# Transposes of the reciprocal row sums issued one step later in both batches of a sliding-window attention, with the broadcast load and the normalisation behind them in the second

## The chip, the cores and the metric

The kernel runs on one core of one Trainium2 chip. The metric is the device time of one execution in microseconds (us). The kernel before takes 372.78 us, the median of 3 runs (372.46 to 373.1).

## The reference

Three blocks are chained: attention with a sliding window and four sink columns, an MLP with a convolution over three tokens and a gate, and attention in four experts weighted by a top-2 gate. The change touches the first block alone, where B=2, H=8, S=768, D=64 and the window is 128:

```python
scores = scale * np.matmul(q, k.transpose(0, 1, 3, 2))
keep = is_sink | in_window
scores = np.where(keep, scores, -1000000000.0)
scores = scores - np.max(scores, axis=-1, keepdims=True)
a = np.exp(scores)
a = a / (np.sum(a, axis=-1, keepdims=True) + 1e-09)
return np.matmul(a, v)
```

Its output x, as (2, 768, 512), goes into the MLP: `h = relu(x @ w_in)`, the convolution over three neighbouring tokens, `h * sigmoid(conv)`, and `@ w_out`.

## The kernel before, in words

The attention works on tiles of 128 queries (`qt`, six to a batch) and pairs of heads (`pr`, four to a tile), so 24 steps to a batch. Each step sends one pair through a chain of stages. Each stage is a small method that issues instructions, and a table gives its lag in steps. `run_phases` (L46) puts the call of stage i at step floor(lag + i times rate) and issues the calls step by step; inside a step the table `ORD1` (L78) sets the order of the stages. Batch 0 is phase `a0`, batch 1 is phase `a1` and begins 24 steps later at a rate of 1.1 steps to a pair; from step 30 on the MLP (stages `m.*`) runs between its steps. Each engine works through its own queue strictly in the order of issue, so the tables set the order of the work on TensorE (PE), VectorE (DVE), ScalarE (ACT), GpSimd (POOL), and on SyncE (SP), which issues the DMAs.

For each pair the stages are:
- S (`a1_S`, L449): matmuls of the scores (L484, in batch 1 L471), mask and minimum on DVE (L486), exponentials on ACT with the row sums into the tile `su` (L489).
- T (L532): PE transposes P (L545), and ACT copies the result into PT (L501).
- V (L576): matmuls of PT with v (L587) into a bank of PSUM that the tile's four pairs share; the sink columns are added by L595, after a transpose L567, a copy SPT (L569) and a product on DVE (L574).

Once for each tile of queries:
- r (L494): 1/(row sum + eps) on DVE, L496 and L497.
- rT (L511): PE transposes `su`, 128x8, into 8x128 (L514); ACT (batch 0, L501) or DVE (batch 1, L503) copies it to the tile rT; a DMA stores it to `rD` in DRAM (L518).
- rB (L520): two loads, L525, read `rD` back, spread over the 128 partitions, into the tile R.
- xm (`x_norm`, L527): DVE multiplies the output in PSUM by R (L529), which frees that bank.
- xh (L611), xl (L614) and halo (L619): the normalised x is split into two parts, xh by a cast on ACT (L501) and xl on DVE (L617), and POOL fills the edges (L623, L626). The MLP's first matmuls, L753, read both parts.

The MLP's stages are H (L753, with the relu's eviction L756 on ACT), the convolution (L766, L767 on DVE, the sigmoid L769 on ACT), the gate (L774 on DVE, L776 on ACT, the product g on POOL, L782) and Y (L797). In the background, whenever a step has credit for it, weights are decoded on DVE (L343, L346, L349, L413, L509) and ACT (L339, L507), and L372 loads the raw weights, 512 KB each, through SP.

PSUM is handed out as eight banks. A new tile gets the bank that has been free for longest and waits for its last reader.

The line that the change touches is the table of lags, L74, one row to a batch. Its first column is the lag of r, and its columns 8 to 13 are the lags of rB, rT, xm, xh, xl and halo, in this order:

```python
LAGS = ((1, 2, 1, 4, 3, 4, 5, 5, 2, 7, 7, 9, 11), (1, 1, 2, 6, 3, 4, 5, 3, 2, 5, 6, 7, 7))
```

Of the kernel before, what the change touches and what calls it, by code (L numbers as in the profile page):

```python
# [70 lines left out]
BG0 = 550  # L71
BG1 = 650
BG2 = 1200
LAGS = ((1, 2, 1, 4, 3, 4, 5, 5, 2, 7, 7, 9, 11), (1, 1, 2, 6, 3, 4, 5, 3, 2, 5, 6, 7, 7))  # L74
LAGM = (1, 2, 3)
A2_N = 2
EVT = 'aaadadada'
# [11 lines left out]
class Kernel:  # L89
# [1033 lines left out]
    def program(self, general):  # L1123
# [5 lines left out]
        with ExitStack() as ctx:  # L1129
# [34 lines left out]
            else:  # L1164
# [18 lines left out]
                self.fixed()  # L1183
                first = [self.attn_phase(b, b * NSTEP, LAGS[b], self.attn_misc(b)) for b in range(B)]
                m1 = NSTEP + MLP_START
# [109 lines left out]
```

## Time and profile before

| | |
|---|---|
| median of 3 runs | 372.78 us (372.46 to 373.1) |
| the profiled execution | 372.33 us, of which the profile's span is 370.5 us |
| PE busy | 359.5 us, 97% of the span |
| DVE busy | 272.3 us, 73% |
| ACT busy | 264.3 us, 71% |
| POOL busy | 118.5 us, 32% |

The profile is of one execution; its times are in us from the span's start. Attention of batch 0 fills the stretch to about 60 us, that of batch 1 runs beside the MLP until about 170 us, and the MoE attention follows behind the MLP. A row of a timeline reads: start, duration, engine, line, operation, the tile written and the tiles read, count, and in brackets how long the engine had been idle and on what it had waited.

### The profile page before, as it was taken

The numbers are of one execution on the slowest core, as the hardware profiler recorded it, in microseconds if no ns is written. First come the engines' busy times: TensorE is split into PE (matmuls) and PEld (weight loads), VectorE is DVE, ScalarE is ACT, GpSimd is POOL, SyncE is SP. The second block draws the span as 40 slices with busy tenths as digits, with TensorE's granted clock in tenths as the row PEclk, the third lists the DMA queues.
The fourth block names the chain that finished last, engine by engine and source line by source line (L and its number), as shares of the span: only waits on it lengthen the run. The fifth ranks groups of instructions, "written<-read, shape, count | busy, mean of one in ns | idle before, by whom it ended". The sixth has DMA issues, their size and how long they took to land.

```text
span 370.5 us, 8892 instructions
## 1 busy us (share of the span) xinstructions
PE 359.5 (97%) x3166; PEld 331.7 (90%) x3166; DVE 272.3 (73%) x834; ACT 264.3 (71%) x778; POOL 118.5 (32%) x230
## 2 busy tenths in 40 slices
PE   7999999899999999999999999999999999999995
PEld 5687877899899999999999999999999899978984
DVE  5689899999887997878756756139668688578631
ACT  4999998766886766546746866249888698759841
POOL 7014120444432442844421222500034144406310
PEclk9999999999999999999999999999999999999999
DMA  7944765353342300001211010000000000001102
GB/s 181 355 138 131 243 208 181 115 189 125 105 125 70 104 30 31 9 21 29 59 44 44 1 58 3 0 2 0 2 3 1 30 30 28 31 1 58 59 32 93
DMA packets 20404, 27.53 MB, mean 74 GB/s; under 512 B 2080, under 2 KB 12928, under 8 KB 20352
## 3 DMA queue, kind: packets, MB, share of 16 engines
q1 hardware_dynamic: 19120, 26.22, 22.3%
q10 hardware_dynamic: 1232, 0.66, 0.8%
q8 instruction: 27, 0.44, 0.5%
q14 instruction: 25, 0.20, 0.2%
HBM read 23.68 MB, written 3.19 MB: 73 GB/s over the span
## 4 chain that ended last, share of the span: by engine, by line
PE 73%; DVE 14%; ACT 6%; issue 2%; POOL 2%; DMA 1%; ACTq 0%; DVEq 0%
PE psB L797 15%; PE psB L753 14%; PE psB L947 9%; PE psB L1071 5%; PE psB L875 5%; PE psB L1047 4%; PE psB L587 4%; PE psB L1095 3%; PE psB L484 3%; PE psB L545 3%; DVE P L486 3%; PE psB L1010 2%; PE psB L1009 2%; PE psB L471 2%; ACT P L489 2%
## 5 line engine op out<-in xcount | busy, mean ns | idle before, releaser
L797 PE MATMUL psB<-g,wouthf 128*128 128x256 f32 x384 | 70.6, 281 | 0.2 <-POOL g L782 0.2
L797 PEld LDWEIGHTS psB<-g,wouthf 128*128 128x128 f32 x384 | 58.9, 188 | 0.6 <-POOL g L782 0.4
L1035 POOL TENSOR_SCALAR P<-P,r 128x256 f32<-128x256 f32 (+5 forms) x48 | 30.1, 640 | 82.8 <-DVE r L1033 42.1
L753 PE MATMUL psB<-xh,winhf 128*128 128x258 f32 x192 | 56.6, 295 | 0.0
L753 PE MATMUL psB<-xh,winlf 128*128 128x258 f32 x192 | 54.2, 282 | 0.0
L753 PE MATMUL psB<-xl,winhf 128*128 128x258 f32 x192 | 54.2, 282 | 0.0
L797 PE MATMUL psB<-g,woutlf 128*128 128x256 f32 x192 | 53.8, 280 | 0.0
L489 ACT ACTIVATE P<-P,nm 128x260 f32<-128x260 f32 (+2 forms) x96 | 46.4, 485 | 10.1 <-DVE nm L486 9.8
L782 POOL TENSOR_TENSOR g<-ht,g 128x256 fp32r<-128x256 f32 x48 | 33.1, 690 | 52.5 <-ACT g L776 46.9
L769 ACT ACTIVATE ht<-ht 128x256 f32<-128x256 f32 x48 | 20.1, 418 | 28.3 <-DVE ht L767 28.2
L774 DVE SCALAR_TENSOR_TENSOR ht<-ht 128x256 f32<-128x256 f32 x48 | 24.2, 505 | 18.8 <-ACT ht L769 18.8
L753 PEld LDWEIGHTS psB<-xh,winhf 128*128 128x128 f32 x192 | 36.4, 189 | 0.3 <-ACT ht L756 0.2
L753 PEld LDWEIGHTS psB<-xl,winhf 128*128 128x128 f32 x192 | 36.5, 190 | 0.0
L753 PEld LDWEIGHTS psB<-xh,winlf 128*128 128x128 f32 x192 | 36.2, 189 | 0.0
L797 PEld LDWEIGHTS psB<-g,woutlf 128*128 128x128 f32 x192 | 36.2, 189 | 0.0
L760 POOL TENSOR_SCALAR ht<-ht,cw 128x256 f32<-128x256 f32 x24 | 15.0, 626 | 59.8 <-ACT ht L756 52.3
L1020 ACT ACTIVATE P<-P,nm 128x256 f32<-128x256 f32 (+3 forms) x48 | 26.8, 561 | 4.7 <-DVE nm L1014 4.6
L767 DVE SCALAR_TENSOR_TENSOR ht<-ht,cw 128x256 f32<-128x256 f32 x48 | 28.3, 589 | 1.7
L545 PE MATMUL psB<-ident,P 128*128 128x128 f32 x176 | 29.1, 281 | 0.3 <-ACT P L489 0.2
L947 PE MATMUL psB<-yh,wqh 128*128 128x256 f32 x96 | 27.2, 283 | 0.0
L947 PE MATMUL psB<-yl,wqh 128*128 128x256 f32 x96 | 27.0, 281 | 0.0
L947 PE MATMUL psB<-yh,wql 128*128 128x256 f32 x96 | 26.9, 280 | 0.0
(176 smaller groups left out, 975.8 us busy)
## 6 DMA issues: line engine op xcount, KB each, us to landing
raw<-in_w_in_dram SPq DMA_DIRECT2D x8, 512.0 KB, 4.2
raw<-in_w_out_dram SPq DMA_DIRECT2D x8, 512.0 KB, 3.3
v<-in_v_dram SPq DMA_DIRECT2D x12, 256.0 KB, 4.2
R<-rD SPq DMA_DIRECT2D x24, 128.0 KB, 3.0
out_dram<-ot SPq DMA_DIRECT2D x11, 256.0 KB, 2.0
k<-in_k_dram SPq DMA_DIRECT2D x7, 260.0 KB, 3.9
raw<-in_wqkv_dram SPq DMA_DIRECT2D x8, 193.0 KB, 3.3
q<-in_q_dram SPq DMA_DIRECT2D x6, 256.0 KB, 3.6
```

The costliest lines, as they stand in the source:

```text
L489: nc.scalar.activation(Pt[:, j, :N], Pt[:, j, :N], AF.Exp, bias=nmx[:, j : j + 1], scale=-1.0, accum_out=sums[:, j : j + 1])
L545: nc.tensor.transpose(ps[:, j, c, :], Pt[:, j, c0 : c0 + P], self.ident)
L753: nc.tensor.matmul(ps[:, :XW], w[:, f, kc, :], x[:, kc, :], start=(i == 0), stop=(i == len(ops) - 1))
L767: nc.vector.scalar_tensor_tensor(t1, h[:, 2 : 2 + CH], self.cw[:, 2 * NF + f : 2 * NF + f + 1], t1, op0=ALU.mult, op1=ALU.add)
L769: nc.scalar.activation(t1, t1, AF.Tanh)
L774: nc.vector.scalar_tensor_tensor(t1, t1, 1.0, h[:, 1 : 1 + CH], op0=ALU.add, op1=ALU.mult)
L782: eng.tensor_tensor(g[:, 1], t1, g[:, 0].bitcast(F32), op=ALU.subtract)
L797: nc.tensor.matmul(self.m1y[d // 2][:, d % 2, :], w[:, f, d, :], g[:, k], start=(first and i == 0 and d % 2 == 0), stop=(last and i == 2), ...
L875: nc.tensor.matmul(ps[:, :NVG], y[:, kc, ts_], w[:, kc, c0 : c0 + NVG], start=(i == 0), stop=(i == len(ops) - 1))
L947: nc.tensor.matmul(ps, w[:, kc, c0 : c0 + P], y[:, kc, :], start=(i == 0), stop=(i == len(ops) - 1))
L1020: nc.scalar.activation(Pt[:, lo:hi], src, AF.Exp, bias=nm[:, 0:1], scale=sg, accum_out=sums[:, j, i : i + 1])
L1035: nc.gpsimd.tensor_scalar(Ps[j][:, :N], Ps[j][:, :N], r[:, j : j + 1], 1.0, op0=ALU.mult, op1=ALU.mult)
```

## The change

One line, seven numbers. In batch 0 the lag of rT goes from 2 to 3. In batch 1 rB goes from 3 to 4, rT from 2 to 3, xm from 5 to 6, xh from 6 to 7, xl from 7 to 8 and halo from 7 to 8. No instruction is added or taken away.

```diff
-LAGS = ((1, 2, 1, 4, 3, 4, 5, 5, 2, 7, 7, 9, 11), (1, 1, 2, 6, 3, 4, 5, 3, 2, 5, 6, 7, 7))
+LAGS = ((1, 2, 1, 4, 3, 4, 5, 5, 3, 7, 7, 9, 11), (1, 1, 2, 6, 3, 4, 5, 4, 3, 6, 7, 8, 8))
```

On PE, in batch 0, around the transpose of the third tile's sums (`su_349`). Before:

```order
L484 MATMUL psB_507<-k_128,q_122 128x260
L514 MATMUL psB_516<-ident,su_349 8x128
L545 MATMUL psB_522<-ident,P_468 128x128 x4
L484 MATMUL psB_533<-k_128,q_122 128x260
L484 MATMUL psB_534<-k_128,q_122 128x260
L587 MATMUL psB_477<-PT_458,v_140 64x128 x2
```

and now:

```order
L484 MATMUL psB_507<-k_128,q_122 128x260
L545 MATMUL psB_516<-ident,P_468 128x128 x4
L484 MATMUL psB_527<-k_128,q_122 128x260
L484 MATMUL psB_528<-k_128,q_122 128x260
L587 MATMUL psB_477<-PT_458,v_140 64x128 x2
...
L514 MATMUL psB_546<-ident,su_349 8x128
```

The transpose L514 has moved behind four transposes of P, the scores of the next pair and its products with v.

On SP, where the fifth tile's reciprocals go to DRAM and come back (`rD_784` before, `rD_818` now); v, k, q and raw are loads for later steps. Before:

```order
L518 DMA rD_784<-rT_782 8x128
L280 DMA v_793<-in_v_dram 128x512
L255 DMA k_859<-in_k_dram 128x520
L525 DMA R_883<-rD_784 64x4x128 x2
```

and now:

```order
L280 DMA v_787<-in_v_dram 128x512
L518 DMA rD_818<-rT_816 8x128
L255 DMA k_859<-in_k_dram 128x520
L525 DMA R_883<-rD_818 64x4x128 x2
```

The store has moved behind a load of v; the two loads of R stand where they stood.

On ACT, in batch 1 beside the MLP, where the second tile's x is cast (`xh`) and a transposed P is copied (`PT_1520` before, `PT_1519` now). Before:

```order
L489 ACTIVATE P_1497,su_1499<-P_1497,nm_1498 128x260 x2
L501 CAST xh_1244<-R_1290 128x4x128
L769 ACTIVATE ht_1410<-ht_1410 128x256
L501 COPY PT_1520<-psB_1515 128x512
```

and now:

```order
L489 ACTIVATE P_1496,su_1498<-P_1496,nm_1497 128x260 x2
L769 ACTIVATE ht_1410<-ht_1410 128x256
L501 COPY PT_1519<-psB_1514 128x512
...
L501 CAST xh_1313<-R_1354 128x4x128
```

The cast has moved from ahead of the copy PT to the next step, behind that step's exponentials.

## Rows read from the trace of the kernel before

**Rows 1.** The page's first part: busy time, share, instructions of each engine.

```profile
PE 359.5 (97%) x3166; PEld 331.7 (90%) x3166; DVE 272.3 (73%) x834; ACT 264.3 (71%) x778; POOL 118.5 (32%) x230
```

**Rows 2.** Windows: stretch, sum; busy us (count) of PE, PEld, DVE, ACT, POOL; clock, DMA, GB/s.

```profile
36.00:45.00 9.00, 8.77 (x73) 6.93 (x72) 8.11 (x29) 8.46 (x29) 2.00 (x10) 1.00 0.66 209
...
60.00:72.00 12.00, 11.04 (x108) 9.78 (x106) 11.05 (x32) 9.51 (x30) 4.75 (x8) 1.00 0.48 153
72.00:90.00 18.00, 17.96 (x169) 16.59 (x170) 17.24 (x41) 11.63 (x36) 7.39 (x16) 1.00 0.45 147
90.00:110.00 20.00, 19.43 (x186) 17.83 (x185) 17.60 (x51) 16.25 (x48) 8.39 (x19) 1.00 0.35 113
```

**Rows 3.** Waits of PE over the span: waited for, us in total, times, longest.

```profile
PE psB L514 <- DVE su L497: 1.7, 4, 1.0
...
PE psB L587 <- ACT PT L501: 0.6, 1, 0.6
...
PE psB L797 <- POOL g L782: 0.2, 1, 0.2
```

**Rows 4.** Timeline of PE at three of the transposes L514.

```profile
36.85 0.27 PE L514 MATMUL psB<-ident,su 128*8 128x128 f32 x1 [0.23 <-DVE su L497]
...
58.94 0.27 PE L514 MATMUL psB<-ident,su 128*8 128x128 f32 x1 [0.30 <-DVE su L497]
...
71.96 0.27 PE L514 MATMUL psB<-ident,su 128*8 128x128 f32 x1 [0.96 <-DVE su L497]
```

**Rows 5.** The chain that ended last, 44 to 97 us: start, us, what.

```profile
52.79 0.01 DVEq L486
...
54.48 0.60 DVE R L529
...
61.48 0.20 DVE rT L503
...
95.82 0.66 PE psB L587 x8
```

**Rows 6.** The operations on su and rT: line, engine, count, ns minimum/median/maximum.

```profile
L514 PE MATMUL psB<-ident,su x12: 269/272/273, 12.7 to 152.6; 128*8 128x128 f32 x12
L503 DVE COPY rT<-psB x6: 272/272/274, 61.4 to 154.0; 8x128 f32<-8x128 f32 x6
```

**Rows 7.** Timelines of ACT, SP and DVE: batch 0's fifth tile.

```profile
46.72 0.24 ACT L501 COPY rT<-psB 8x128 f32<-8x128 f32 x1
46.98 0.29 SPq L518 DMA_DIRECT2D rD<-rT  x1
48.87 0.24 ACT L569 CAST SPT<-psB 128x128 fp32r<-128x128 f32 x1
49.82 1.25 SPq L525 DMA_DIRECT2D R<-rD  x2
54.40 0.69 DVE L529 TENSOR_TENSOR R<-psB,R 128x512 f32<-128x512 f32 x1
```

**Rows 8.** Waits of SP: waited for, us in total, times, longest.

```profile
SPq L525 <- DMA rD<-rT: 10.2, 9, 1.9
```

**Rows 9.** The page's DMA issues: count, KB each, median us to landing.

```profile
R<-rD SPq DMA_DIRECT2D x24, 128.0 KB, 3.0
```

**Rows 10.** Timelines of ACT and DVE at three places of batch 1.

```profile
71.67 0.50 ACT L489 ACTIVATE P<-P,nm 128x260 f32<-128x260 f32 x1
...
94.37 0.61 ACT L501 CAST xh<-R 128x512 fp32r<-128x512 f32 x1
...
95.19 0.57 ACT L501 COPY PT<-psB 128x512 f32<-128x512 f32 x1
...
152.29 1.78 DVE L617 TENSOR_TENSOR xl<-R,xh 128x512 fp32r<-128x512 f32 x1
```

**Rows 11.** Timeline of SP: the third tile's store and the loads behind it.

```profile
30.40 0.30 SPq L518 DMA_DIRECT2D rD<-rT  x1
31.75 1.25 SPq L525 DMA_DIRECT2D R<-rD  x2
```

## The prediction

> **What bounds the kernel now.** I read the busy shares first. PE is busy for 97% of the span [rows 1], so the most that a reordering can win is the little idle time that PE has, and the most that it can lose is what it adds to it. The windows say where that idle time lies [rows 2]. Batch 0's attention at 36 to 45 us keeps PE busy 8.77 of 9 us, with DVE at 8.11 and ACT at 8.46 close behind: three engines are nearly full there, and a stall of any of them has little room to be made good. From 60 to 72 us, where the MLP joins in, PE is busy 11.04 of 12 us and DVE 11.05. After that PE is full: 17.96 of 18, then 19.43 of 20. The granted clock is 1.00 in all of these windows, the level of 2.4 GHz, so no term here comes from the clock.
>
> Next come the waits of PE [rows 3]. The longest group is the transpose that the change moves: L514 waits for the reciprocals L497, four times, 1.7 us in all. The timeline shows three of them, 0.23, 0.30 and 0.96 us [rows 4]. Further down are a wait of 0.6 us for a copy PT at L587 and one of 0.2 us at L797.
>
> Last I read the chain of waits from 44 to 97 us [rows 5]. Up to 52.79 us it runs on PE. There it passes to DVE, and from there to 95.82 us nearly all of it is work of DVE, some of ACT, among it the product L529 at 54.48 and the copy of rT at 61.48. So the transposes that PE waits for at 58.94 and 71.96 are not what sets the end: there DVE is late as such, and PE would wait for it at the next instruction too.
>
> **The change, term by term.** No instruction is added, so no engine gets more work. Each sum below is made against the profiled execution, 372.33 us. That is 0.45 us under the median of the three timed runs and 0.13 us under the fastest, so I set the difference that comes out on the median.
>
> (a) The transpose at 36.85 us, in batch 0 [rows 4]. A step later its reciprocals are long done. The instruction then next on PE is the transpose of P, of a pair whose exponentials are further on. The wait of 0.23 us goes, and as the chain is PE's up to 52.79 us it reaches that point. I take -0.2; the bounds are 0 (P's exponentials as late as the sums) and -0.23.
>
> (b) The way of batch 0's reciprocals through DRAM gets a step less. rT moves, rB and xm do not. Take the fifth tile [rows 7]: the copy of rT ends its step at 46.72 us, and the store is issued 0.26 later, at 46.98. In the new order the copy stands on ACT just ahead of the copy SPT of the next step, which now starts at 48.87, so the store comes at about 48.87 + 0.26 = 49.1 us. The loads can be issued when the store has landed. Shown are 1.35 us from store to load, at 30.40 and 31.75 [rows 11], and 2.84 us, at 46.98 and 49.82 [rows 7]; SP's nine waits for the store, 10.2 us in all and 1.9 us at most [rows 8], say that the store's landing is what sets this. The loads would thus start at 50.5 to 52.0. The second of the two starts 0.6 us later, half of the 1.25 us that both take, and lands 3.0 us after its issue [rows 9]: at 54.1 to 55.6 us. The product L529 starts at 54.40 now, and by (a) could start at 54.2. It would thus wait between nothing and 1.4 us, on DVE, where the mask of the next pair (L486) and the decode of weights stand behind it, and this is the chain's own stretch [rows 5]. A wait of 0.3 us is what I take, nearer to the low end, because one load, of k, will be issued close behind this store where it was two, v and k, and the store of rows 11, the quick one, had none behind it but its own. From the place of before that is +0.1 us, with (a) spent; the bounds of (a) and (b) together are -0.2 and +1.2. The Trainium skill, "DMA: Bandwidth & Descriptors", section "Anatomy of one DMA", gives some 2.0 us as the fixed cost of a DMA and says that most of it is the confirmation of the write, longest in HBM. By an estimate from that page, 2.0 us for the store, R would land at 54.7 or 54.8 and the product would wait 0.5 to 0.6 us, so that (a) and (b) would come to +0.4 instead of +0.1; the 1.35 us of the trace is under the page's figure and the 2.84 above it.
>
> (c) Batch 1's copy of rT leaves the chain at 61.48 us [rows 5], where it counts 0.20 us, and goes behind the product L529 at 63.49 or so, and with it the store, which nobody waits for yet. I take -0.2; its whole duration, 0.272 us [rows 6], is one bound and 0 the other, if DVE does not catch the time up.
>
> (d) The waits at 58.94 and 71.96 us [rows 4]. Behind each stands a transpose of P, which needs the exponentials of its own pair. At 71.96 the last of these starts at 71.67 and takes 0.50 us [rows 10], to 72.17, so PE would wait for it till then in any order. Of 0.30 and 0.96 I take -0.1 in all, from 0 to -0.3.
>
> (e) At 95.82 us PE waits 0.6 us for PT [rows 3]. ACT does the cast xh first, at 94.37 for 0.61 us, and then the copy, at 95.19 [rows 10]. In the new order xh goes behind the copy, a step later, so the copy is 0.5 us or so earlier and the wait goes. But between 90 and 110 us PE is idle for only 20 - 19.43 = 0.57 us, which is this wait: DVE, with 17.60, and ACT, with 16.25 [rows 2], still have to do the same work ahead of the next matmuls L753, and the cast comes when that work comes. So most of it returns a few us later. I take -0.1, between 0 and -0.6.
>
> (f) Near 152 us a late xl on DVE, 1.78 us long [rows 10], stands ahead of the convolution; PE waits at L797 for 0.2 us [rows 3]. xl goes a step later: -0.2, between 0 and -0.2.
>
> In batch 1 the loads of R and the product move together with rT, so the time between store and product is as it was; the bank of PSUM that the product frees is held for a step longer, which costs nothing as long as PE finds a free bank, and PE shows no wait for a bank in rows 3. POOL's halo moves with xl, and POOL is busy for 8.39 us of 20 there [rows 2].
>
> Sum: +0.1 - 0.2 - 0.1 - 0.1 - 0.2 = -0.5 us, so 371.8 for the profiled execution and 372.3 on the median. About 0.2%, or 0.75 us, is what a measurement of this kernel can tell from no change, so the forecast is a small gain that does not show.
>
> **The rivals.**
>
> *The waits of PE really go* (faster). If the four waits at L514 and those at L587 and L797 are the last ones where they stand, and nothing is late behind them, the gain is 0.23 + 0.96 + 0.57 + 0.2 = 2.0 us, to 370.8 on the median; half of it, 1.0 us, gives 371.8. For it speaks that L514 is the longest group of waits and that after 72 us PE is full, so what reaches PE there is kept. Against it speaks the chain, on which these waits are DVE's and ACT's lateness.
>
> *The reciprocals come back too late* (slower). The mechanism is (b) alone: DVE stands at L529 in front of work that does not need R. It decides from the point where the store takes longer than about 1.5 us to land, since then R is later than 54.2 us; at 2.84 us it costs 1.2 us against the place of before, on the chain, and with only (c) to set against it the kernel takes 1.0 us more, 373.8 on the median. Every tile of batch 0 loses the same step, so that more than one such wait is possible. The rule on overlap in the Trainium skill, "DMA: Bandwidth & Descriptors", section "Rules for kernel authors", is to issue a DMA early and to wait for it late; in batch 0 this change issues later and waits at the same place. No run yet shows which of the two durations of the store the new place has.
>
> *Nothing but a place changes* is part of the forecast: by (d) the transposes of P take over the waits, and if (a), (c), (e) and (f) are each at their weak end it is 372.8.
>
> **How the numbers follow.** The forecast gets 0.45; its own range is 371.9 to 373.4, from the sum with (c) to (f) a little larger to (b) at its high end with (c) to (f) at half. The gain in PE's waits gets 0.33, for the size of the group in rows 3. The late reciprocals get 0.22. Of the forecast 0.04 is faster by over 0.75 us and 0.02 slower; of the rivals nearly all lies on its own side. That makes 0.36 faster, 0.41 within 0.2%, and 0.23 slower. The range goes from 371.2, somewhat short of the whole gain in PE's waits, to 373.7, somewhat short of the full price of a late R.
>
> **What would show it.** In the profile after, the waits of L514 for L497 should be gone, and L545 should wait for the exponentials at about 59 and 72 us. The product L529 at 54 us should show an idle time of DVE of some tenths of a us that ends with a load of R; over 1 us there, and more of it at the other tiles of batch 0, and the slower case holds. At 61 us no copy of rT should stand on the chain. At about 95 us PE should not wait for PT, but shortly after for DVE or ACT. If instead PE's idle time between 52 and 110 us has shrunk by more than 1 us and none of it comes back, the forecast is wrong on the fast side.

## The result, and the profile after

The change makes the kernel slower: 375.16 us, the median of 12 runs (373.85 to 379.35), against 372.85 us before (372.46 to 373.1, 12 runs); ratio 1.0076, 95% interval 1.0051 to 1.0101. (The ratios here are those on record with their intervals; they are close to the quotients of the medians, here 1.0062, but not the same.) That is outside the range of the prediction and on the side it gave 0.23. The runs also spread over 5.5 us, where those before spread over 0.64 us. The profiled execution took 376.84 us, of which the span is 375.0 us: 4.5 us more than the one profiled before (372.33 us) and above its own median, so its trace shows the losses somewhat larger than they are on the median.

The page's first part, after:

```profile
PE 361.7 (96%) x3166; PEld 332.8 (89%) x3166; DVE 272.0 (73%) x834; ACT 265.3 (71%) x778; POOL 120.1 (32%) x230
```

DVE, ACT and POOL have the work that they had [rows 1]; PE is busy 2.2 us longer with the same 3166 instructions, and its span grows by 4.5 us, so in this execution about half of the loss is new idle time and half is the same work done slower. The windows of the same stretches, and one more, say where:

```profile
36.00:45.00 9.00, 8.49 (x72) 6.71 (x71) 8.31 (x31) 8.53 (x29) 2.02 (x9) 1.00 0.62 206
...
60.00:72.00 12.00, 12.00 (x105) 10.55 (x104) 10.57 (x31) 8.93 (x30) 3.87 (x6) 0.86 0.51 171
72.00:90.00 18.00, 17.94 (x171) 16.58 (x169) 17.24 (x43) 12.65 (x38) 6.16 (x13) 1.00 0.36 119
90.00:110.00 20.00, 18.60 (x176) 16.83 (x175) 17.96 (x51) 15.74 (x48) 9.14 (x19) 1.00 0.38 126
150.00:170.00 20.00, 18.92 (x174) 18.38 (x173) 14.59 (x28) 10.04 (x27) 12.30 (x17) 1.00 0.05 15
```

and the last of these stretches before the change:

```profile
150.00:170.00 20.00, 19.82 (x181) 19.29 (x180) 15.24 (x22) 9.21 (x24) 12.67 (x18) 1.00 0.05 15
```

From 90 to 110 us PE is busy 18.60 of 20 us where it was 19.43 [rows 2]; from 150 to 170 us 18.92, where it was 19.82. From 60 to 72 us it is busy throughout, but at a granted clock of 0.86. The waits of PE after:

```profile
PE psB L797 <- POOL g L782: 1.1, 1, 1.1
...
PE psB L753 <- ACT PT L501: 1.0, 1, 1.0
PE psB L471 <- DMA q<-in_q_dram: 0.9, 1, 0.9
PE psB L595 <- DVE SPT L574: 0.7, 1, 0.7
...
PE psB L587 <- DMA v<-in_v_dram: 0.5, 1, 0.5
```

The group that the change aimed at, L514 waiting for L497 with 1.7 us [rows 3], is gone. Five waits stand in its place. Two of them, for v and q, are waits for loads that the kernel before had in time; a third such wait, 0.4 us for a q at 17.09 us, stands further down the list.

The timeline of DVE at the product L529 in batch 0, after (first, third and fifth tile):

```profile
23.50 0.69 DVE L529 TENSOR_TENSOR R<-psB,R 128x512 f32<-128x512 f32 x1 [0.85 <-DMA R<-rD]
...
40.16 0.69 DVE L529 TENSOR_TENSOR R<-psB,R 128x512 f32<-128x512 f32 x1 [0.50 <-DMA R<-rD]
...
56.73 0.69 DVE L529 TENSOR_TENSOR R<-psB,R 128x512 f32<-128x512 f32 x1 [1.05 <-DMA R<-rD]
```

DVE stands idle for R three times, 2.4 us in all; before it did so nowhere. The fifth tile's product starts at 56.73 instead of 54.40 us [rows 7]. The timeline of SP, after, for the third tile's loads of R and what stands behind them, and for the fifth tile:

```profile
36.23 1.25 SPq L525 DMA_DIRECT2D R<-rD  x2
...
38.97 0.55 SPq L372 DMA_DIRECT2D raw<-in_w_out_dram  x1
39.58 0.43 SPq L280 DMA_DIRECT2D v<-in_v_dram  x1
...
50.00 0.29 SPq L518 DMA_DIRECT2D rD<-rT  x1
...
53.02 1.25 SPq L525 DMA_DIRECT2D R<-rD  x2
54.30 0.60 SPq L271 DMA_DIRECT2D q<-in_q_dram  x1
```

Store to load takes 3.02 us for the fifth tile, and the load of q (L271), which stands behind the loads of R in SP's order, is issued at 54.30 instead of 51.11. PE waits 0.89 us for a q at 57.96. For the third tile the loads of R are issued at 36.23 instead of 31.75 [rows 11], and 512 KB of raw weights behind them at 38.97 instead of 36.41, now right ahead of a load of v; PE waits 0.51 us for v at 43.58. SP itself stands longer for the stores than before, 14.7 us in all and 3.6 us at most, where it was 10.2 and 1.9 us [rows 8]:

```profile
SPq L525 <- DMA rD<-rT: 14.7, 8, 3.6
```

So one late store holds up two things: DVE at L529, and on SP every load behind L525, which then come in a bunch. Both are on the chain that ended last, 20 to 120 us:

```profile
19.37 4.11 DMA R<-rD
...
39.58 3.96 DMA v<-in_v_dram
...
53.66 2.98 DMA R<-rD
```

The chain of before has no load of R and no load of v in this stretch.

Windows of 2 us, after:

```profile
56.00:58.00 2.00, 1.11 (x11) 0.61 (x9) 1.27 (x3) 1.34 (x8) 0.00 (x0) 1.00 0.98 331
58.00:60.00 2.00, 1.25 (x13) 1.06 (x14) 1.94 (x8) 1.42 (x7) 0.00 (x0) 1.00 0.98 350
60.00:62.00 2.00, 2.00 (x13) 1.50 (x13) 1.71 (x8) 1.47 (x6) 0.00 (x0) 0.52 0.25 95
62.00:64.00 2.00, 2.00 (x13) 2.00 (x13) 1.59 (x7) 1.36 (x6) 0.00 (x0) 0.62 0.50 136
```

and before:

```profile
56.00:58.00 2.00, 1.65 (x17) 1.27 (x16) 1.91 (x8) 1.73 (x7) 0.00 (x0) 1.00 0.97 268
58.00:60.00 2.00, 1.70 (x16) 1.32 (x17) 1.41 (x7) 1.74 (x7) 0.00 (x0) 1.00 0.46 152
60.00:62.00 2.00, 2.00 (x21) 1.74 (x21) 1.97 (x8) 1.36 (x7) 0.00 (x0) 1.00 0.83 224
```

After, PE is busy 2.36 of 4 us from 56 to 60, and then the granted clock is 0.52 and 0.62: much of these 4 us was at the level of 1.2 GHz. Before, PE was busy 3.35 of 4 us there (1.65 and 1.70) and the clock stayed at 1.00. At 0.52 and 0.62 PE did in 4 us the work of 2.3, so the clock took about 1.7 us of this execution, as much as it lies above the median. The median itself does not hold this loss: the mean granted clock of the whole run is 0.994 here and 0.991 in one other of the 12 runs, and 0.997 to 1.000 in the remaining ten, the slowest of all (379.35 us, 0.998) among them; the profiled run before has 0.999.

### The profile page after: what moved, and what is told of

The parts are those of the page before. It is cut to its first block, busy times and chain, and to the rows that moved or that the text cites. A ratio compares the mean times of both kernels' runs of the same rounds, so it can differ in the third digit from the quotient of the medians.

```text
span 375.0 us, 8886 instructions
## 1 busy us (share of the span) xinstructions
PE 361.7 (96%) x3166; PEld 332.8 (89%) x3166; DVE 272.0 (73%) x834; ACT 265.3 (71%) x778; POOL 120.1 (32%) x230
## 4 chain that ended last, share of the span: by engine, by line
PE 69%; DVE 12%; ACT 8%; DMA 5%; issue 3%; POOL 2%; SPq 0%; ACTq 0%; DVEq 0%
PE psB L797 15%; PE psB L753 14%; PE psB L947 9%; PE psB L1071 5%; PE psB L875 5%; PE psB L1047 5%; PE psB L1095 4%; ACT P L489 3%; PE psB L587 3%; PE psB L1010 2%; DVE P L486 2%; PE psB L1009 2%; PE psB L471 2%; DMA R<-rD 2%; PE psB L545 2%
## 5 line engine op out<-in xcount | busy, mean ns | idle before, releaser
L774 DVE SCALAR_TENSOR_TENSOR ht<-ht 128x256 f32<-128x256 f32 x48 | 23.1, 481 | 18.1 <-ACT ht L769 18.1
L545 PE MATMUL psB<-ident,P 128*128 128x128 f32 x176 | 30.2, 286 | 0.6 <-ACT PT L501 0.2
L767 DVE SCALAR_TENSOR_TENSOR ht<-ht,cw 128x256 f32<-128x256 f32 x48 | 28.4, 591 | 1.7
L766 DVE SCALAR_TENSOR_TENSOR ht<-ht,cw 128x256 f32<-128x256 f32 x48 | 27.2, 566 | 0.1
```

The lines of the kernel that those rows point to most:

```text
L545: nc.tensor.transpose(ps[:, j, c, :], Pt[:, j, c0 : c0 + P], self.ident)
L766: nc.vector.scalar_tensor_tensor(t1, h[:, 0:CH], self.cw[:, f : f + 1], t1, op0=ALU.mult, op1=ALU.add)
L767: nc.vector.scalar_tensor_tensor(t1, h[:, 2 : 2 + CH], self.cw[:, 2 * NF + f : 2 * NF + f + 1], t1, op0=ALU.mult, op1=ALU.add)
L774: nc.vector.scalar_tensor_tensor(t1, t1, 1.0, h[:, 1 : 1 + CH], op0=ALU.add, op1=ALU.mult)
```

## The experiments

Two theories stood against each other, and a third between them. Theory 1: batch 0 is the price, since R comes back too late for a normalisation that was not moved. Theory 2: batch 1 is, where the normalisation and the split of x move. Theory 3: both.

**Halves.** Batch 0's lag alone, and batch 1's six lags alone.

```diff
-LAGS = ((1, 2, 1, 4, 3, 4, 5, 5, 2, 7, 7, 9, 11), ...
+LAGS = ((1, 2, 1, 4, 3, 4, 5, 5, 3, 7, 7, 9, 11), ...
```

> Only batch 0's transpose is a step later (its lag 2 to 3); batch 1 as before. Theory 1 (the reciprocals of batch 0 come back too late, and DVE and SP stand waiting for them): this run carries most of the slowdown, 374.3 to 375.5 us against 372.85 before, with waits of DVE at the product L529 for loads of R at 23, 40 and 56 us of 0.5 to 1.1 us each, and late loads of v and q behind the stores on SP. Theory 2 (batch 1's later casts and banks cost the time): 372.3 to 373.2 us. Theory 3 (both halves alike): about 374.0 us.

Measured: 373.70 us against 372.46, ratio 1.0033 (1.0017 to 1.0049), near theory 3. Of the waits expected for theory 1, two at L529 came, longer than expected, and none at the third tile; PE waits for no v and no q here, so SP's part does not show in this profile. DVE at L529 in this run:

```profile
24.37 0.69 DVE L529 TENSOR_TENSOR R<-psB,R 128x512 f32<-128x512 f32 x1 [1.72 <-DMA R<-rD]
...
56.73 0.69 DVE L529 TENSOR_TENSOR R<-psB,R 128x512 f32<-128x512 f32 x1 [1.17 <-DMA R<-rD]
```

```diff
-... (1, 1, 2, 6, 3, 4, 5, 3, 2, 5, 6, 7, 7))
+... (1, 1, 2, 6, 3, 4, 5, 4, 3, 6, 7, 8, 8))
```

> Only batch 1's six lags are a step later; batch 0 as before. Theory 1: 372.0 to 373.2 us, PE's waits of 0.30 and 0.96 us at L514 replaced by shorter ones for exponentials, no wait at L529 in batch 0. Theory 2: 374.0 us or more, with the waits of about 1.0 us for PT near 93 us and for g near 158 us that the changed kernel shows. Theory 3: about 374.0 us.

Measured: 374.14 us against the same 372.46, ratio 1.0044 (1.0030 to 1.0059). Theory 3 holds: 0.33% and 0.44% make the 0.76% of the whole, within their intervals. The profiled executions of the two halves are the slowest of their runs, 2.0 and 1.4 us above the medians, so their waits too are larger than on the median. The waits foretold for theory 2 are there (0.97 us for PT at 92.29, 1.1 us for g). In the profiled execution of this run batch 0, which is as before, shows a late R too. SP:

```profile
46.99 0.29 SPq L518 DMA_DIRECT2D rD<-rT  x1
...
51.09 1.25 SPq L525 DMA_DIRECT2D R<-rD  x2
```

The store is issued where it was before, 46.99 against 46.98, but the loads come 4.10 us later instead of 2.84 [rows 7], and L529 waits 1.06 us. So the landing of this store differs from one execution to the next by more than a us, with nothing changed ahead of it.

**Batch 1, which part.** Transpose and loads alone (rT 3, rB 4), and normalisation, cast, xl and halo alone (6, 7, 8, 8).

> Batch 1's transpose and broadcast loads a step later (lags of rT 2 to 3, rB 3 to 4); normalisation, cast xh, xl and halo stay, as does batch 0. Theory A (in batch 1 the price is the split of x, that is the product L529, the cast and xl, which a step later stand ahead of the convolution on DVE): 372.0 to 372.9 us, no wait of about 1 us for g near 158 us. Theory B (the price is the copy of rT on DVE, or R coming late): 373.3 to 374.3 us.

> Batch 1's normalisation, cast xh, xl and halo a step later; its transpose and loads stay, as does batch 0. Theory A: 373.5 to 374.3 us, with waits of about 1.0 us for PT near 92 us and for g near 157 us, and xl on the chain near 103 and 144 us. Theory B: 372.2 to 372.9 us.

Measured against 372.76: 373.18 us, ratio 1.0013 (1.0003 to 1.0022), and 374.25 us, ratio 1.0035 (1.0022 to 1.0049). Theory A: the normalisation with the split of x carries the larger part. Two points missed: the first run lies between the ranges of the two theories, and in the second the wait for PT is 0.5 us and not 1.0. On the transposes' waits, the run with rT and rB alone shows PE at the places of [rows 4]:

```profile
59.03 0.93 PE L545 MATMUL psB<-ident,P 128*128 128x128 f32 x4 [0.27 <-ACT P L489]
...
71.87 0.93 PE L545 MATMUL psB<-ident,P 128*128 128x128 f32 x4 [0.70 <-ACT P L489]
```

0.30 and 0.96 us for the sums have become 0.27 and 0.70 us for the exponentials. The 0.3 us won there is not kept; the run as a whole is 0.13% slower, and what takes it back is not shown.

The chain of the run with all of batch 1's lags names what is in the way, 92 to 160 us:

```profile
102.84 0.60 DVE xl L617
103.44 0.19 DVE rT L503
...
144.50 0.60 DVE xl L617
...
153.77 2.39 POOL yl L819 x2
```

xl stands on DVE ahead of the convolution L766, L767, on which the sigmoid, the gate and POOL's product g depend; at 153.77 POOL's yl (L819) stands ahead of g as well. The next runs move xl behind the convolution in each step, by the order table. Everything else keeps its lags, and the order on PE, ACT, POOL and SP is that of the run it is compared with.

```diff
-ORD1 = '... a1.sV a1.xl a1.r a0.S a1.halo a0.sL ... m.conv m.misc a0.xh'
+ORD1 = '... a1.sV a1.r a0.S a0.sL ... m.conv a1.xl a1.halo m.misc a0.xh'
```

> Batch 1's normalisation, cast, xl and halo a step later, as in the run with these alone (374.25 us there), but in each step xl and halo come behind the convolution L766 and L767 in place of ahead of it. If xl ahead of the convolution is the price: 372.4 to 373.3 us, no xl on the chain near 103 and 144 us and no wait of 1 us for g near 157 us. If the bank held longer or the cast xh on ACT is the price: 374.0 us or more.

Measured: 372.33 us against 372.73, ratio 0.9993 (0.9984 to 1.0002). The 0.35% is gone with that one move on DVE. Its windows, and behind them those of the run with xl ahead:

```profile
90.00:110.00 20.00, 19.63 (x190) 18.07 (x190) 17.93 (x48) 16.21 (x49) 8.15 (x18) 1.00 0.39 129
150.00:170.00 20.00, 19.89 (x183) 19.36 (x182) 15.07 (x26) 9.29 (x24) 13.16 (x18) 1.00 0.05 15
```

```profile
90.00:110.00 20.00, 19.03 (x182) 17.30 (x181) 17.81 (x47) 15.25 (x45) 7.79 (x17) 1.00 0.37 125
150.00:170.00 20.00, 19.03 (x177) 18.50 (x176) 14.21 (x24) 10.30 (x27) 12.96 (x17) 1.00 0.05 15
```

PE has 19.63 and 19.89 of 20 us, against 19.03 in both stretches with xl ahead. One part of the expectation missed: an xl of 0.60 us is still on the chain, at 144.38; no wait of PE of 1 us for g follows it.

> The kernel before with batch 1's xl and halo behind the convolution in each step: the control for the run before this, and a candidate. If xl costs nothing where it stands before: 372.2 to 372.8 us. If the wait for g at 154 us and the xl on the chain near 70 and 80 us are its doing: 371.5 to 372.2 us.

Measured: 372.97 us against the same 372.73, ratio 1.0005 (0.9992 to 1.0018). In the kernel before, xl stands where it costs nothing that can be told.

> Only batch 1's six lags a step later, with xl and halo behind the convolution; batch 0 as before. If xl ahead of the convolution is all of batch 1's price: 372.2 to 373.2 us, against 374.1 for the same lags without this. If the later copy of rT on DVE has a price of its own, as the run with rT and rB alone hints (0.13%): 372.8 to 373.3 us.

Measured: 373.20 us against 372.52, ratio 1.0014 (1.0003 to 1.0025). Of batch 1's 0.44%, xl's place makes 0.30%; what is left, 0.14%, is close to what rT and rB alone cost, 0.13%.

> The changed kernel whole, with batch 1's xl and halo behind the convolution in each step. If the two halves add up, as the runs with one half each say, this takes batch 1's part away and leaves batch 0's: 373.3 to 374.2 us against 375.2 for the changed kernel, with the waits of DVE at L529 in batch 0 and none of 1 us for g. If the halves don't add up: 375 us.

Measured: 374.00 us (372.28 to 377.11), ratio 1.0041 (1.0018 to 1.0064). The halves add up: 0.76% less xl's 0.30% is near 0.41%. The spread of 4.8 us stays, so it goes with batch 0's half: the run with that half alone spreads over 3.2 us, the one before this, with batch 0 as it was, over 2.3. In its profile PE waits for the v that there too follows the raw weights, 40.00 after 39.39, behind a waiting L525 (36.65):

```profile
44.98 0.88 PE L587 MATMUL psB<-PT,v 128*64 128x128 f32 x12 [1.75 <-DMA v<-in_v_dram]
```

> Batch 1's transpose alone, half a step later: behind the next step's transposes of P in place of ahead of them, with the loads of R still in the same step, and no other lag changed. If the waits of 0.30 and 0.96 us at L514 near 59 and 72 us were worth having: 371.0 to 372.2 us. If the exponentials behind them take the waits over, as in the run with batch 1's transpose a whole step later: 372.4 to 373.3 us.

```diff
-ORD1 = 'm.rest a0.more a1.T a0.gather ... a0.r a1.rT m.conv ...
+ORD1 = 'm.rest a0.more a1.T a1.rT a0.gather ... a0.r m.conv ...
```

(with rT's lag at 3). Measured: 372.45 us against 372.73, ratio 1.0002 (0.9992 to 1.0011). PE waits 0.28 and 0.72 us at the same two transposes of P. The waits of L514 were worth nothing that can be told: the 0.26 us that the two places have less is within the interval.

**Batch 0: is it R?** Half a us instead of a step, with the transpose behind the same step's transposes of P:

```diff
-... a0.halo a0.rT a1.xm a1.misc a1.xh a0.sT a0.T a0.misc ...
+... a0.halo a1.xm a1.misc a1.xh a0.sT a0.T a0.rT a0.misc ...
```

> Batch 0's transpose keeps its lag of 2 but is issued behind the same step's transposes of P instead of ahead of them, some 0.5 us later on PE; batch 1 as before. If R's way through DRAM is the price and half a us of it is to be had: the wait of 0.23 us at 36.85 goes, R is not late but perhaps by 0.1 to 0.3 us at 22 and 54 us, 372.4 to 373.0 us. If any delay of R costs its full length at these two places: 373.3 us or more.

Measured: 373.10 us against 372.46, ratio 1.0014 (1.0004 to 1.0023). Half a us later costs 0.14%, a whole step 0.33%. In its profile no L529 waits; PE waits 0.44 us for v at 42.72 us instead, and that load, issued at 39.63, is on its chain for 3.04 us.

Then R was made later by another way, with the order as it was before: the stores and loads issued from POOL's queue.

```diff
-        self.nc.sync.dma_start(self.a1L[(b, qt)], rT)
+        (self.nc.sync if b else self.nc.gpsimd).dma_start(self.a1L[(b, qt)], rT)
```

(and the same in `a1_rB`)

> The kernel before with batch 0's stores L518 and loads L525 issued from POOL's queue: the control for the run before this. If SP's waits cost nothing in the kernel before: 372.2 to 372.8 us. If POOL's way of issuing brings R later by a us or so: 373 us or more, with waits of DVE at L529 near 22 and 54 us, where R has least to spare.

> Batch 0's transpose a step later, as in the run with that alone (373.70 us there), and its stores L518 and loads L525 are issued from POOL's queue in place of SP's, so that no load of q, k, v or raw weights stands behind them. If late loads behind SP's waits are a good part of the price: 372.6 to 373.2 us, and no wait of PE for q or v. If the price is DVE standing at L529 for R: 373.5 to 374.5 us, with the same waits at L529 of 1.1 to 1.7 us.

Measured: 374.34 us, ratio 1.0052 (1.0031 to 1.0073), and 383.59 us, ratio 1.0289 (1.0267 to 1.0311), against 372.76. With POOL's queue R comes later than with SP's, so the second is no test of SP; both say what a late R costs with nothing behind it on SP. POOL's own work now stands behind these issues instead, up to 3.95 us at a time for a store in the first. DVE in the first:

```profile
23.99 0.69 DVE L529 TENSOR_TENSOR R<-psB,R 128x512 f32<-128x512 f32 x1 [1.42 <-DMA R<-rD]
...
49.80 0.69 DVE L529 TENSOR_TENSOR R<-psB,R 128x512 f32<-128x512 f32 x1 [1.88 <-DMA R<-rD]
```

With 0.36 us at the sixth tile that is 3.7 us of waiting in an execution of 375.92 us, 3.2 us above before; in the second, the waits of DVE at L529 sum to 13.2 us (8.2 for R, and 5.0 for which the profile names no releaser) in one of 386.83 us, 14.1 above. By these two, an estimate, a us of waiting at L529 goes with about a us of time; it is not the price of R alone, since POOL's work and the clock, which falls to 0.50 in windows of 2 us of both executions, are in it.

Last, R was given its time back by moving the normalisation as well, in three ways.

> As the run with batch 0's transpose alone a step later, but its normalisation and cast xh are a step later too (lags 7 to 8), so that R has its old time to come back. If the price is DVE standing at L529: no wait for R, and 372.4 to 373.2 us. If the price is SP, whose later loads of q, k and v stand behind the store and the loads of R: the same time as the run without this, within 0.5 us, with PE still waiting for q or v at 43 and 58 us. A bank of PSUM held for a step longer may cost up to 1 us; then PE's waits name L529.

> Batch 0's transpose a step later, and its normalisation L529 some 1.2 us later on DVE (behind the decode of weights, ahead of the next step's masks and ahead of the next tile's first products with v), with the cast xh a step later. If the price of the late transpose is DVE standing at L529 for R: waits there of at most 0.5 us and 372.4 to 373.2 us. If the bank of PSUM that L529 frees decides, as in the run with a whole step: 374.5 us or more, with PE waiting for exponentials near 30 us and for L529.

Measured: 378.13 us against 372.46, ratio 1.0148 (1.0133 to 1.0162), and 381.07 us against 372.73, ratio 1.0210 (1.0189 to 1.0231). Neither tells: no L529 waits, and no wait of PE names the bank that L529 frees, but both edits put the cast xh so late that DVE stands at xl, as here in the first:

```profile
27.49 1.40 DVE L617 TENSOR_TENSOR xl<-R,xh 128x512 fp32r<-128x512 f32 x1 [1.73 <-ACT xh L501]
```

The third moves xl as well:

```diff
-LAGS = ((1, 2, 1, 4, 3, 4, 5, 5, 2, 7, 7, 9, 11), ...
+LAGS = ((1, 2, 1, 4, 3, 4, 5, 5, 3, 8, 8, 10, 11), ...
-ORD1 = '... a1.r a0.S ... a0.sV a0.xm a1.more ...
+ORD1 = '... a1.r a0.xm a0.S ... a0.sV a1.more ...
```

> Batch 0 as in the run with its normalisation 1.2 us later, but xl a step later still (lag 9 to 10): in that run DVE stood at xl for the cast xh, 0.8 to 2.3 us at a time, which the edit itself had caused. If R's lateness at L529 is batch 0's price: no wait at xl, at most 0.5 us at L529, 372.4 to 373.4 us. If the later place of the normalisation costs by itself (its bank of PSUM, DVE's work ahead of the masks): 374 us or more.

Measured: 374.98 us against 372.52, ratio 1.0063 (1.0046 to 1.0081), so as a whole it misses. (Four of its six runs have a granted clock of 0.992 or 0.993; the other two took 374.18 and 374.87 us.) Its trace is of use. No L529 waits, and up to 60 us the loss is away: the decode L343 that waits for ACT stands at 60.32 us here, at 62.38 with batch 0's transpose alone (in that kernel's slowest execution), and at 60.03 in the kernel before.

```profile
60.32 0.43 DVE L343 TENSOR_SCALAR f64u<-f64u 128x512 int32<-128x512 int32 x1 [0.60 <-ACT f64u L339]
```

What it loses comes behind that. The chain, from 62 us, and ACT's timeline of the same place:

```profile
62.08 4.37 DMA raw<-in_w_out_dram
```

```profile
66.47 0.67 ACT L339 ACTIVATE f64u<-raw 128x512 f32<-128x512 f32 x1 [0.67 <-DMA raw<-in_w_out_dram]
```

These raw weights are issued by SP at 62.08 us, behind the sixth tile's loads of R at 60.72, which had waited for their store of 56.44. So for batch 0 both parts of theory 1 are seen at work, DVE at L529 and SP behind L525: with R given its time the first is gone and the second still costs. No run takes away the second alone, and how the 0.33% divides between them is open.

**A version that may beat both**: batch 1's transpose half a step later, with xl behind the convolution.

> A candidate: batch 1's transpose half a step later, its loads of R in the same step, normalisation, cast, xl and halo a step later, xl and halo behind the convolution; batch 0 as before. The two parts alone gave a ratio of 1.0002 and 0.9993. If they add up: 372.2 to 372.7 us, no difference that can be told; under 372.0 would be a gain.

Measured: 372.63 us against 372.52, ratio 0.9998 (0.9988 to 1.0007). No gain that can be told; the kernel before stands.

## Why the prediction was wrong, by its own steps

The forecast was -0.5 us. Measured was +2.3 on the medians. The steps that failed are (b), the time of R's way through DRAM in batch 0, and (e) with (f), the place of xl in batch 1; the mechanism that the second rival named is the first of them, somewhat under half of the loss.

- **What bounds.** Right in one point that the sum then left out: that batch 0's three engines are nearly full and that a stall of any of them has little room to be made good [rows 2]. The sum counted one tile's R. That no term comes from the clock held for the median, not for the profiled execution.
- **(a)** held in that no wait of L514 is left. Whether its 0.2 us was won is not shown: the first tile's product had by then stood 0.85 us for R.
- **(b)** is the step that failed first. The range of 1.35 to 2.84 us from store to load came from two tiles of one execution, and the sixth tile of that same execution, which the prediction leaves out, took 3.69 us (store issued at 54.69, loads at 58.38, after 1.6 us in which SP waited for the store). Measured were 3.02 us for the fifth tile of the changed kernel, 4.32 us for its sixth, and 4.10 us in a run where nothing around that store was changed. The store itself came at 50.00 and not 49.1 us (the kernel was by then 0.9 us behind before: the fourth tile's product starts at 48.10 instead of 47.17), and the wait of 0.3 us at the fifth tile was 1.05. "Nearer to the low end", by the loads issued behind the store, rested on two rows and did not hold: the third tile's store, with the same order around it, took 1.35 us in the run with batch 0's transpose alone and 3.01 us in the changed kernel. And two costs were missing. The same step is lost at every tile, and two more of them waited (0.85 and 0.50 us); the rival says so in words and prices one. And SP stands at L525 too: q, v and raw weights behind it came late or in a bunch, 0.9 and 0.5 us of PE's waits. The prediction asked what is queued behind L529 on DVE and never what is queued behind L525 on SP. The price of the whole step, in the run with batch 0 alone, was +1.2 us where (a) and (b) had +0.1, at the upper end of their bounds.
- **(c)** won nothing that can be seen: rT is off the chain at 61 us, as forecast, but in the changed kernel it stands on it at 82.80 and 104.63 us, where before it stood at 61.48 and 76.92. (c) and (d) together were forecast as -0.3 us; transpose and loads alone cost 0.13%, some 0.4 us, and which of the two costs it is open.
- **(d)** held as to the place: 0.3 us less at the two places in that run, with the exponentials as the next thing that is late. With the half step the whole is 1.0002, so that no gain reached the end that can be told.
- **(e)** was forecast as -0.1. The wait for PT at 95.82 did go, but another for PT stands at 93.48, 1.01 us long, and from 90 to 110 us PE lost 0.83 us more than before (19.43 to 18.60) instead of less. The prediction says that the moved work "comes when that work comes" and takes most of the gain for returned; what comes is xl, ahead of a convolution, and it takes more than was won.
- **(f)** was forecast as -0.2, on the ground that xl goes a step later and so out of the way at 152 us. It is an order that repeats: xl then stands ahead of the next step's convolution. The wait for g went from 0.2 to 1.1 us. (e) and (f) together, forecast as -0.3 us, came out 0.35%, some 1.3 us, slower in the run with these lags alone, and xl's place behind the convolution gives 0.30% to 0.42% back.

Of the rivals, the late R was right in kind and place, and the sign that the prediction set for it came: over 1 us at the fifth tile and more at others. Its price of 1.2 us for one wait is near the 1.2 us of batch 0's half, but that half had two waits or more and SP's late loads in it, so the match is luck. The gain in PE's waits failed as the chain said it would; its sum of 2.0 us, said to be of four waits at L514, holds only two of them (all four, 1.7 us, would have made 2.5). The slower half in batch 1 was no rival at all. The Trainium skill, "DMA: Bandwidth & Descriptors", section "Rules for kernel authors", says to issue a DMA early and to wait for it late; batch 0's half, which only issues later, is 0.33% slower, and so agrees. The 2.0 us of the same page's section "Anatomy of one DMA" is given there for DMAs issued from GpSimd, and the stores here are issued from SyncE. It lies between the 1.35 and the 4.32 us from store to load that single stores showed here; the stores issued from POOL, with the order of before, took 3.0 us to land, as a median. So no one figure would have carried the step.

## What to carry to other kernels

A wait of the busiest engine is worth what the next late thing behind it leaves, here nothing that could be told, so look first at what that engine would wait for in the next instruction. When a step that starts a transfer is moved and its user is not, count the slack at each use, take the slowest landing that the trace shows and not a middle one, and ask of each queue, the one that issues DMAs too, what stands behind the instruction that will wait. A work item moved by a step does not leave the critical engine: see what it stands ahead of in its new step, and move it inside the step first.

## What the runs showed that was not expected

The time from a 4 KB store to the load that needs it was 1.35 to 4.32 us in different places and executions, beside loads of q, k, v and raw weights; 2.84 and 4.10 us are the same store at the same time in the same order, and so are 1.35 and 3.01 us but for 0.84 us in time. The kernels whose batch 0 has no slack left for this also spread more: over 5.5, 4.8 and 3.2 us in 12 runs each, where the kernel before spread over 0.64 us in 12 runs, and over 1.3 to 2.4 us in other sets of 23 to 29. That the store's time makes the spread is likely but not shown.

The granted clock fell within the attention of batch 0: after stretches in which PE was busy 1.11 and 1.25 of 2 us it was 0.52 and 0.62 in the next two, and 1.00 again after that. It did not always fall at this place: in the changed kernel with xl moved, PE was busy 1.08 and 1.73 of 2 us there and the clock stayed at 1.00, and in ten of the changed kernel's 12 runs the mean clock is 0.997 or more. In an execution where it falls, a stall of DVE costs not only the time that PE stands, but also speed in the stretch behind it, where PE had work.
